# Strassen products of g @ w_out that add on in PSUM over several products, in another order, with the last tile copied in halves

## Chip, cores and metric

The kernel runs on one core of a Trainium2 chip. The metric is the device time of one execution in microseconds. Before the change it was 564.1 us, the median of three runs (562.77, 564.2 and 564.1 us).

## The reference

Attention with a capped score, then two two-layer networks one behind the other. Shapes: q, k, v are 2 x 12 x 448 x 64; x is 896 x 768, each w_in 768 x 2048, each w_out 2048 x 768 (held as 64-bit floats).

```
scores = cap * tanh(q @ k.T / 8 / cap)
attn   = softmax(scores);  x = attn @ v            # heads side by side: 896 x 768
h = x @ w_in1;   g = where(h > 0, h, exp(min(h, 0)) - 1);   x = g @ w_out1
h = x @ w_in2;   g = maximum(0.01 * h, h);                  out = g @ w_out2
```

## The kernel before

Everything runs transposed: an activation tile is 128 features x 448 tokens, one of two batches. Each fp32 operand is split into a high and a low part that TensorE takes in its fp32r format, and a product is three matmuls: high x high, high x low, low x high. ScalarE (ACT) makes the high part by a copy with rounding (`rounded`, L303), VectorE (DVE) the low part by a subtraction (`remainder`, L306).

The work has three stages: attention (pairs of heads, to some 116 us), then for each network the hidden layer (`hidden`, L632: 16 tiles of 128 features, 36 matmuls each at L646) and the output layer (`products`, L726).

The output layer is one level of Strassen's scheme in Winograd's form. g is cut into four quarters B11 to B22 (feature half x batch; 8 tiles of 128 features each), w_out into A11 to A22 (4 slabs of 128 x 768 each). Seven products of sums of quarters take the place of eight. Each product has 8 steps kt of 9 matmuls (3 output tiles m x 3 parts, L751), so 72 matmuls; a network has 504 of them.

- Names. `tl1.6.0` is the low part of B's operand in network 1, product 6, step 0; `th1.6.0` its high part; `S1.6.0l` and `S1.6.0h` the parts of A's operand (one for two steps). `gg1.3.0` is a tile of g (tile 3, batch 0), `w1.10.0` a slab of w_out (quarter A21, slab 0). `u` tiles hold sums of products, `c` tiles a finished quarter of the result.
- Operands. `operand` (L710) has DVE add or subtract two quarters in place (L718), 16 times on slabs and 32 times on g tiles for each network.
- Accumulators. Each product opens its own (`accumulators`, L610): a pair of PSUM banks `acc` for m = 0, 1 (tag `sc`, two of them) and one bank `acs` for m = 2 (tag `po`, two of them). So two products can be open at a time, and the third reopens the banks of the first.
- After a product (`after`, L771), for each m: products 7 and 1 are copied by ACT into u7 and u1 (L777); product 6 gives u2 = u1 + M6 and u7 = u7 + u2 (L781, L784); 5, 3, 4 and 2 give a quarter each by a DVE addition (L790), and 5 also u2 = u2 + M5 (L794). In network 1 a quarter is split into the parts `xh2`, `xl2` for the next hidden layer; in network 2 it is transposed on TensorE (`ct`, L809), copied out of PSUM and stored.
- The order of the products is 7, 1, 6, 5, 3, 4, 2. In the last one the last two steps are done m by m, so that the first tiles finish early.
- `convert` (L542) makes fp32 weights of the 64-bit ones; two of its steps are on ACT (L555, L567) and two on DVE (L576, L585).

No engine chooses its work at run time. `Plan` (L18) takes every piece with a cost, what it reads and writes and a due time, lists them engine by engine in an order worked out beforehand, and `order` (L73) hands them out; each engine then runs its own list strictly in turn and waits for semaphores where a piece needs another engine's result. Where two engines touch one PSUM tile, their accesses are kept apart by such a wait, two reads too.

Of the kernel before, what the change touches and what calls it, by code (L numbers as in the profile page):

```python
# [256 lines left out]
def block(ctx, tc, consts, q, k, v, w_in1, w_out1, w_in2, w_out2, out, bounded):  # L257
# [17 lines left out]
    P = 128  # L275
# [266 lines left out]
    def convert(key, src, name, tag, due):  # L542
# [16 lines left out]
        def low():  # L559
# [7 lines left out]
            nc.scalar.activation(x, top, AF.Identity, scale=1.0 / 32.0, bias=third)  # L567
# [64 lines left out]
    def hidden(nm, m, at):  # L632
# [76 lines left out]

    def operand(nm, p, side, idx):  # L710
        spec = PRODUCTS[p][side]
        if len(spec) == 1:
            return part(nm, side, spec[0], idx)
        x, op, y, to = spec
        x, y, to = (part(nm, side, pr, idx) for pr in (x, y, to))

        def fn():
            nc.vector.tensor_tensor(out=V[to], in0=V[x], in1=V[y], op=op)  # L718

        plan("DVE", (0.87, 0.54)[side], fn, reads=[x, y], writes=[to], port=True)  # L720
        return to
# [4 lines left out]
    def products(nm, T0):  # L726
        for j, p in enumerate(PRODUCTS):
            tags, where = accumulators(list(range(MS)))
            T = T0 + j * MS * 3 * (KF // 2) * MM
            s_of, t_of = {}, {}  # L730
            for kt in range(KF // 2):
# [10 lines left out]
                def fn(kts=(kt,), ms=range(MS), tags=tags, where=where, nm=nm, p=p):  # L742
                    if 0 in kts:
# [24 lines left out]
            for m in range(MS):  # L768
                after(nm, p, m, where[m], T + (KF // 2) * 9 * MM - (6 * MM * (MS - 1 - m) if p == 2 else 0))

    def after(nm, p, m, acc, T):  # L771
# [3 lines left out]
        free = T if p == 2 else T + 7.0  # L775
        if p in (7, 1):
# [10 lines left out]
        i, n, of, op = {2: (0, 0, 1, ADD), 3: (0, 1, 2, ADD), 4: (1, 0, 7, SUB), 5: (1, 1, 7, ADD)}[p]
        c = f"c{nm}.{i}{n}.{m}"
        home = "x" if p == 5 else "g"
        plan("DVE", 0.54, lambda: nc.vector.tensor_tensor(  # L790
            out=tl(home, home, c, [P, S]), in0=V[u(of)], in1=bank(acc), op=op),
            reads=[u(of), acc], writes=[c], new={c: home}, due=free + 2)
        if p == 5:
            plan("DVE", 0.54, lambda: nc.vector.tensor_tensor(out=V[u(2)], in0=V[u(2)], in1=bank(acc), op=ADD),  # L794
                 reads=[u(2), acc], writes=[u(2)], due=free + 3)
# [145 lines left out]
```

## Time and profile before

| | |
|---|---|
| timed runs | 562.77, 564.2, 564.1 us; median 564.1 us |
| profiled execution, first to last instruction | 560.4 us |
| median less that span | 3.7 us |
| TensorE (PE) busy | 550.4 us, 98% |
| weight loads (PEld, beside PE) | 452.7 us, 81% |
| DVE busy | 479.8 us, 86% |
| ACT busy | 385.8 us, 69% |

The profiled execution's own time is not listed beside its span; what a timed run has beyond the span lies before the first and after the last instruction. The granted TensorE clock is 1.00 in every window but the last (0.87 from 546 us on, where PE runs out of work), which is the 2.4 GHz level. Busy shares say which engine is full, not which one is waited for: DVE is busy for all of 238 to 280 us, and whether TensorE waits for it is seen in the waits.

### The profile page before, as it was taken

The numbers are of one execution on the slowest core, as the hardware profiler recorded it, in microseconds if no ns is written. First come the engines' busy times: TensorE is split into PE (matmuls) and PEld (weight loads), VectorE is DVE, ScalarE is ACT, GpSimd is POOL, SyncE is SP. The second block draws the span as 40 slices with busy tenths as digits, with TensorE's granted clock in tenths as the row PEclk, the third lists the DMA queues.
The fourth block names the chain that finished last, engine by engine and source line by source line (L and its number), as shares of the span: only waits on it lengthen the run. The fifth ranks groups of instructions, "written<-read, shape, count | busy, mean of one in ns | idle before, by whom it ended". The sixth has DMA issues, their size and how long they took to land.

```text
span 560.4 us, 7414 instructions
## 1 busy us (share of the span) xinstructions
PE 550.4 (98%) x2750; PEld 452.7 (81%) x2750; DVE 479.8 (86%) x628; ACT 385.8 (69%) x539; POOL 52.5 (9%) x32
## 2 busy tenths in 40 slices
PE   8999999999999999999999999999999999999995
PEld 4333433489999999999999999999999999999994
DVE  2699999987887999999999977888997599997662
ACT  5899999919877889865566766776775256555550
POOL 2544454500000000000000000000000000000000
PEclk9999999999999999999999999999999999999998
DMA  8933641155777667400012128676672000001103
GB/s 159 245 77 82 141 137 34 57 159 144 220 215 222 174 210 225 123 2 0 1 56 57 57 65 250 193 224 195 205 206 72 0 2 1 1 1 49 50 20 86
DMA packets 61436, 61.90 MB, mean 110 GB/s; under 512 B 23248, under 2 KB 53200, under 8 KB 61392
## 3 DMA queue, kind: packets, MB, share of 16 engines
q1 hardware_dynamic: 61120, 61.23, 39.3%
q8 instruction: 23, 0.38, 0.3%
q14 instruction: 21, 0.17, 0.1%
q10 hardware_dynamic: 240, 0.11, 0.1%
q0 software_dynamic: 32, 0.00, 0.0%
HBM read 58.59 MB, written 2.75 MB: 109 GB/s over the span
## 4 chain that ended last, share of the span: by engine, by line
PE 87%; DVE 5%; ACT 4%; POOL 1%; issue 1%; DMA 1%; SPq 0%; ACTq 0%; POOLq 0%
PE acc L646 29%; PE acc L751 24%; PE acs L751 12%; PE po L496 3%; DVE rec L516 2%; PE sm L510 1%; PE ct L809 1%; DMA firstq<-in_q_dram 1%; PE acs15.0_1845 L646 1%; PE acs38.0_3883 L646 1%; PE acs32.1_3492 L646 1%; PE acs9.1_1437 L646 1%; PE acs35.0_3687 L646 1%; PE acs29.1_3302 L646 1%; PE acs6.1_1242 L646 1%
## 5 line engine op out<-in xcount | busy, mean ns | idle before, releaser
L516 DVE RECIPROCAL rec<-sm 128x448 f32<-128x448 f32 x12 | 35.4, 2949 | 2.4 <-PE sm L510 2.2
L358 DVE COPY kT<-ntk 128x448 f32<-128x448 f32 x12 | 7.4, 619 | 6.7 <-PE ntk L343 6.6
L343 PEld LDWEIGHTS ntq<-ident,nq 112*128 112x128 f32 x44 | 4.3, 141 | 9.3 <-DVE kT L358 8.6
L343 PEld LDWEIGHTS ntk<-ident,nk 112*128 112x128 f32 x44 | 4.3, 141 | 7.3 <-issue 6.7
L354 DVE TENSOR_SCALAR qT<-ntq,qscale 128x448 f32<-128x448 f32 x12 | 8.1, 678 | 1.9 <-PE ntq L343 1.9
L829 ACT COPY ob<-ct 112x512 f32<-112x512 f32 x7 | 4.1, 587 | 7.4 <-PE ct L809 6.9
L343 PE MATMUL ntq<-ident,nq 112*128 112x112 f32 x44 | 6.6, 273 | 1.4 <-DVE kT L358 1.4
L524 DVE TENSOR_TENSOR xf<-po,rec 128x448 f32<-128x448 f32 x12 | 7.5, 623 | 0.4
L567 ACT ACTIVATE rawo1.00.2_972<-rawo1.00.2_972,third 128x768 int32<-128x768 uint8 x1 | 1.0, 1006 | 8.9 <-DMA rawo1.00.2_972<-in_moe_w_out_dram 8.9
L343 PE MATMUL ntk<-ident,nk 112*128 112x112 f32 x44 | 6.6, 273 | 0.0
L675 ACT ACTIVATE ea2.14.0_3955<-acs38.0_3883 128x448 f32<-128x448 f32 x1 | 0.5, 543 | 5.4 <-PE acs38.0_3883 L646 5.4
L303 ACT CAST th2.7.3_4004<-gg2.3.1_3278 128x448 fp32r<-128x448 f32 x1 | 0.6, 567 | 5.0 <-PE acs L751 5.0
L238 PE MATMUL unused<-busy 128*128 128x128 f32 x12 | 2.9, 435 | 1.1 <-DVE third L244 1.1
L391 ACT ACTIVATE e0.0_155<-sc0.0_147 112x896 f32<-112x896 f32 x1 | 0.9, 917 | 3.9 <-PE sc0.0_147 L371 3.9
L238 PEld LDWEIGHTS unused<-busy 128*128 128x128 f32 x12 | 2.6, 330 | 1.1 <-DVE third L244 1.1
L790 DVE TENSOR_TENSOR c2.00.0_4963<-u2.1.0_4297,acc 128x448 f32<-128x448 f32 x1 | 0.6, 622 | 3.2 <-PE acc L751 3.2
L660 ACT ACTIVATE ea1.0.0_1062<-acc 128x448 f32<-128x448 f32 x1 | 0.5, 547 | 4.1 <-PE acc L646 4.1
L827 DVE COPY ob<-ct 112x512 f32<-112x512 f32 x4 | 2.8, 690 | 0.7 <-PE ct L809 0.7
L666 DVE SCALAR_TENSOR_TENSOR gg1.0.0_1074<-ea1.0.0_1062,acc 128x448 f32<-128x448 f32 x1 | 0.6, 620 | 3.2 <-ACT ea1.0.0_1062 L663 3.2
L675 ACT ACTIVATE ea2.13.0_3904<-acc 128x448 f32<-128x448 f32 x1 | 0.5, 543 | 3.9 <-PE acc L646 3.9
L306 DVE TENSOR_TENSOR tl2.7.3_4006<-gg2.3.1_3278,th2.7.3_4004 128x448 fp32r<-128x448 f32 x1 | 0.6, 626 | 3.0 <-ACT th2.7.3_4004 L303 3.0
L263 DVE TENSOR_SCALAR ncap<-capb 128x1 f32<-128x1 f32 x1 | 0.2, 154 | 3.6 <-DMA capb<-in_cap_dram 3.6
(4976 smaller groups left out, 2263.9 us busy)
## 6 DMA issues: line engine op xcount, KB each, us to landing
nv<-in_v_dram SPq DMA_DIRECT2D x12, 224.0 KB, 3.0
nk<-in_k_dram SPq DMA_DIRECT2D x11, 224.0 KB, 3.6
nq<-in_q_dram SPq DMA_DIRECT2D x11, 224.0 KB, 3.8
out_dram<-ob SPq DMA_DIRECT2D x3, 672.0 KB, 4.3
rawg1.0_203<-in_moe_w_in_dram SPq DMA_DIRECT2D x1, 768.0 KB, 7.3
rawg1.1_248<-in_moe_w_in_dram SPq DMA_DIRECT2D x1, 768.0 KB, 6.0
rawg1.2_282<-in_moe_w_in_dram SPq DMA_DIRECT2D x1, 768.0 KB, 7.7
rawo1.00.0_514<-in_moe_w_out_dram SPq DMA_DIRECT2D x1, 768.0 KB, 5.6
```

Source lines behind the costliest of these rows:

```text
L238: nc.tensor.matmul(t, busy, busy, start=True, stop=True)
L343: nc.tensor.matmul(t[:, c * CP : (c + 1) * CP], V[f"n{nm}{n}"][:, c], ident[:CP, :CP], is_transpose=True, start=True, stop=True,)
L354: nc.vector.tensor_scalar(out=t, in0=V[pt][:, :S], scalar1=qscale, scalar2=None, op0=ALU.mult)
L358: nc.vector.tensor_copy(t, V[pt][:, :S])
L496: nc.tensor.matmul(V[po][j * D : (j + 1) * D, :S], V[f"nv{n}"][:, j, c], V[e][:, c % 2, j], start=(c == 0), stop=(c == NC - 1),)
L510: nc.tensor.matmul(t[j * D : (j + 1) * D, :S], ones[:CP], V[f"s{n}.0"][:, j], start=True, stop=True,)
L516: plan("DVE", 2.97, lambda: nc.vector.reciprocal(out=tl("att", "rec", rec, [P, S]), in_=V[sm][:, :S]), reads=[sm], writes=[rec], new={rec: ...
L524: nc.vector.tensor_tensor(out=tl("att", "xf", xf, [P, S]), in0=V[po][:, :S], in1=V[f"rec{n}"], op=ALU.mult)
L646: nc.tensor.matmul(bank(where[b]), V[g + w][:, kt, :], V[f"{part}{nm}.{b}.{kt}"], start=(x == 0 and i == 0), stop=(x == KM - 1 and i == 2),)
L751: nc.tensor.matmul(bank(where[m]), V[sp][:, kt % 2, m * P : (m + 1) * P], V[tp], start=(kt == 0 and i == 0), stop=(kt == KF // 2 - 1 and i ...
L809: nc.tensor.matmul(t[:CP, x * P : (x + 1) * P], V[c][:, x * CP : (x + 1) * CP], ident, is_transpose=True, start=True, stop=True,)
L829: nc.scalar.copy(dst, src)
```

## The change

Products that go into the same sum now share an accumulator, and the sum forms in PSUM. There are three: X takes M1, then M6, then M5, then M3; Y takes M7, then M4 (its operand is now B21 - B12 with the opposite sign, so that it adds); Z takes M2. The order is 1, 7, 6, 4, 5, 2, 3. `opens` says whether a product starts its accumulator or adds on. ACT copies the sum out where a later step needs it: u1 (after product 1), u7 (after 7) and u6 (X after product 6). Then c10 = u6 + Y, c11 = u7 + X, c00 = u1 + Z, each one DVE addition for each m; c01 is X itself after product 3 and needs none. The additions of L781, L784 and L794 are gone.

In network 1 c01 is split into its parts straight from PSUM. In network 2 it is copied out first: m = 0 by ACT, m = 1 by DVE, and m = 2, the last tile, in two halves of 224 columns, one by each. In `convert` the step L567 is now a Copy with a constant for its bias, where it was Identity with the bias read from a tile.

```diff
-            nc.scalar.activation(x, top, AF.Identity, scale=1.0 / 32.0, bias=third)
+            nc.scalar.activation(x, top, AF.Copy, scale=1.0 / 32.0, bias=-15.5 / 32.0)
...
-        7: ((A11, SUB, A21, A21), (B22, SUB, B12, B12)),
-        1: ((A11,), (B11,)),
...
+        1: (A11, (), B11, (), "X"),
+        7: (A21, ((A11, SUB, A21, A21),), B12, ((B22, SUB, B12, B12),), "Y"),
+        6: (A21, ((A22, SUB, A21, A21),), B12, ((B12, ADD, B11, B12),), "X"),
+        4: (A22, (), B12, ((B22, SUB, B12, B11), (B21, SUB, B12, B12)), "Y"),
...
+    FINAL = {4: (1, 0, 6), 5: (1, 1, 7), 2: (0, 0, 1), 3: (0, 1, None)}
+    LAST = 3
...
-            tags, where = accumulators(list(range(MS)))
+            opens = PRODUCTS[p][4] not in sums
+            if opens:
+                sums[PRODUCTS[p][4]] = accumulators(list(range(MS)))
+            tags, where = sums[PRODUCTS[p][4]]
...
-                                    start=(kt == 0 and i == 0), stop=(kt == KF // 2 - 1 and i == 2),
+                                    start=(opens and kt == 0 and i == 0), stop=(kt == KF // 2 - 1 and i == 2),
...
-        if p in (7, 1):
+        if p not in FINAL:
             plan("ACT", 0.46, lambda: nc.scalar.copy(tl("x", "x", u(p), [P, S]), bank(acc)),
...
-            plan("DVE", 0.54, lambda: nc.vector.tensor_tensor(out=V[u(7)], in0=V[u(7)], in1=V[u(2)], op=ADD),
...
-            plan("DVE", 0.54, lambda: nc.vector.tensor_tensor(out=V[u(2)], in0=V[u(2)], in1=bank(acc), op=ADD),
...
+        last = p == LAST and m == MS - 1
+        halves = [(c, 0, S)]
+        if last:
+            halves = [(c + "a", 0, S // 2), (c + "b", S // 2, S)]
+        if of is None:
+            for x, (name, a, z) in enumerate(halves):
+                by = ("ACT", "DVE")[(m + x) % 2]
```

What this does to the lists of the engines is shown at three places. TensorE's list keeps its shape: the same count of matmuls at each line, and the same places at which a step of the next product comes ahead of the last step of the one before; only the operands' names differ.

First DVE in network 1, the stretch that ends with the first low part of the fourth product (product 5 before, product 4 in the change). Before, it reads:

```order
L306 TENSOR_TENSOR tl1.6.4_2324<-gg1.4.1_1294,th1.6.4_2319 128x448
L306 TENSOR_TENSOR S1.6.3l<-w1.10.3_1403,S1.6.3h 128x768
L718 TENSOR_TENSOR w1.10.1_1267<-w1.01.1_1839,w1.10.1_1267 128x768
L306 TENSOR_TENSOR tl1.6.5_2342<-gg1.5.1_1366,th1.6.5_2339 128x448
L718 TENSOR_TENSOR w1.10.2_1331<-w1.01.2_1906,w1.10.2_1331 128x768
L306 TENSOR_TENSOR tl1.6.6_2358<-gg1.6.1_1432,th1.6.6_2353 128x448
L306 TENSOR_TENSOR S1.5.0l<-w1.00.0_607,S1.5.0h 128x768
L718 TENSOR_TENSOR w1.10.3_1403<-w1.01.3_1937,w1.10.3_1403 128x768
L718 TENSOR_TENSOR gg1.0.1_1080<-gg1.0.1_1080,gg1.8.0_1569 128x448
L306 TENSOR_TENSOR tl1.5.0_2390<-gg1.0.0_1074,th1.5.0_2371 128x448
```

Here the additions on slabs of w stand between the parts of product 6. In the change the same stretch reads:

```order
L306 TENSOR_TENSOR S1.6.3l<-w1.10.3_1415,S1.6.3h 128x768
L306 TENSOR_TENSOR tl1.6.5_2335<-gg1.5.1_1378,th1.6.5_2331 128x448
L718 TENSOR_TENSOR gg1.4.0_1300<-gg1.12.1_1825,gg1.4.1_1302 128x448
L718 TENSOR_TENSOR gg1.4.1_1302<-gg1.12.0_1815,gg1.4.1_1302 128x448
L306 TENSOR_TENSOR tl1.6.6_2352<-gg1.6.1_1444,th1.6.6_2347 128x448
L306 TENSOR_TENSOR S1.4.0l<-w1.11.0_1482,S1.4.0h 128x768
L718 TENSOR_TENSOR gg1.5.0_1370<-gg1.13.1_1892,gg1.5.1_1378 128x448
L718 TENSOR_TENSOR gg1.5.1_1378<-gg1.13.0_1888,gg1.5.1_1378 128x448
L718 TENSOR_TENSOR gg1.6.0_1442<-gg1.14.1_1962,gg1.6.1_1444 128x448
L306 TENSOR_TENSOR tl1.4.0_2385<-gg1.0.1_1080,th1.4.0_2365 128x448
```

The additions on slabs of w have moved out of this stretch, and the additions on g for the two operands of product 4 have come in, two for each tile. From the first low part of product 6 to that of the next product DVE has 9 instructions on 768 columns and 13 on 448 before, and 4 and 21 in the change.

Second ACT in network 1, in the fourth product. Before, its list reads:

```order
L303 CAST S1.5.1h<-w1.00.1_813 128x768
L303 CAST th1.5.1_2407<-gg1.1.0_1121 128x448
L303 CAST th1.5.2_2422<-gg1.2.0_1179 128x448
L303 CAST th1.5.3_2438<-gg1.3.0_1219 128x448
L303 CAST S1.5.2h<-w1.00.2_1024 128x768
L303 CAST th1.5.4_2457<-gg1.4.0_1292 128x448
L303 CAST S1.5.3h<-w1.00.3_1135 128x768
```

It holds high parts alone. In the change the list reads:

```order
L303 CAST th1.4.3_2430<-gg1.3.1_1231 128x448
L303 CAST S1.4.2h<-w1.11.2_1627 128x768
L782 COPY u1.6.0_2437<-acc_1975 128x448
L782 COPY u1.6.1_2450<-acc_1975 128x448
L303 CAST th1.4.4_2452<-gg1.4.1_1302 128x448
L303 CAST S1.4.3h<-w1.11.3_1697 128x768
L782 COPY u1.6.2_2457<-acs_1976 128x448
L303 CAST th1.4.5_2470<-gg1.5.1_1378 128x448
```

The three copies u1.6 of accumulator X have come in among the high parts. The buffer `acc_1975` that they read is the one that product 1 opened and that product 5 adds to next.

Third the end of the program, with what each instruction waits for (a suffix _49 belongs to the semaphore's name). ACT's list before is:

```order
L829 COPY ob_4887<-ct_4905 112x4x128 [waits PE_49]
L303 CAST th2.2.6_4934<-gg2.14.0_3959 128x448 [waits DVE_49,PE_49]
L303 CAST th2.2.7_4936<-gg2.15.0_4022 128x448 [waits PE_49,Activation_49]
L829 COPY ob_4985<-ct_4973 112x4x128 [waits DMAHW4_49,PE_49]
L829 COPY ob00.0_4995<-ct_4989 112x256 [waits PE_49]
```

The last two rows copy transposed tiles out of PSUM. In the change ACT's list is:

```order
L303 CAST th2.3.7_4902<-gg2.15.1_4000 128x448 [waits PE_49,Activation_49]
L813 COPY c2.01.0_4929<-acc_3962 128x448 [waits PE_49]
L813 COPY c2.01.2a<-acs_3963 128x224 [waits PE_49]
L844 COPY ob_4953<-ct_4939 112x4x128 [waits DMAHW4_49,PE_49]
L844 COPY ob01.0_4963<-ct_4957 112x256 [waits PE_49]
```

Two copies of the quarter's own tiles have come in ahead of them. DVE's list before is:

```order
L306 TENSOR_TENSOR tl2.2.7_4949<-gg2.15.0_4022,th2.2.7_4936 128x448 [waits PE_49,Activation_49]
L790 TENSOR_TENSOR c2.00.0_4963<-u2.1.0_4297,acc_4837 128x448 [waits PE_49]
L790 TENSOR_TENSOR c2.00.1_4971<-u2.1.1_4310,acc_4837 128x448
L790 TENSOR_TENSOR c2.00.2_4978<-u2.1.2_4321,acs_4838 128x448 [waits PE_49]
L827 COPY ob_4985<-ct_4980 112x4x128 [waits DMAHW4_49,PE_49]
L827 COPY ob00.2_4997<-ct_4989 112x256 [waits Activation_49]
```

Three additions make the quarter's tiles. In the change DVE's list is:

```order
L306 TENSOR_TENSOR tl2.3.6_4913<-gg2.14.1_3945,th2.3.6_4900 128x448 [waits DVE_49,PE_49,Activation_49]
L306 TENSOR_TENSOR tl2.3.7_4915<-gg2.15.1_4000,th2.3.7_4902 128x448 [waits PE_49,Activation_49]
L815 COPY c2.01.1_4937<-acc_3962 128x448 [waits Activation_49]
L815 COPY c2.01.2b<-acs_3963 128x224 [waits Activation_49]
L842 COPY ob_4953<-ct_4948 112x4x128 [waits DMAHW4_49,PE_49]
L842 COPY ob01.2_4965<-ct_4957 112x256 [waits Activation_49]
```

The last quarter's three additions on DVE have become a copy of m = 0 on ACT, one of m = 1 on DVE that waits for ACT, and two halves of m = 2, of which DVE's waits for ACT's. ACT's copy of the transposed tile m = 0 (`ob` from `ct`) now stands behind two copies more.

## Rows read from the trace of the kernel before

**Rows 1.** The page, part 1: busy time, share of the span, instructions.

```profile
PE 550.4 (98%) x2750; PEld 452.7 (81%) x2750; DVE 479.8 (86%) x628; ACT 385.8 (69%) x539; POOL 52.5 (9%) x32
```

**Rows 2.** PE's waits, first and last of six: us in total, times, longest.

```profile
PE ntq L343 <- DVE kT L358: 1.4, 3, 0.7
...
PE ct L809 <- ACT ob L829: 0.2, 1, 0.2
```

**Rows 3.** Windows of 14 us: busy time (instructions), granted clock, DMA share, GB/s.

```profile
core 0: us, PE busy (x) PEld busy (x) DVE busy (x) ACT busy (x) POOL busy (x), PEclk, DMA share, GB/s
...
252.00:266.00 14.00, 14.00 (x70) 12.97 (x70) 14.00 (x23) 8.00 (x15) 0.00 (x0) 1.00 0.00 0
...
476.00:490.00 14.00, 14.00 (x71) 12.97 (x70) 14.00 (x22) 8.14 (x15) 0.00 (x0) 1.00 0.01 1
...
546.00:561.00 15.00, 8.20 (x45) 7.16 (x44) 4.05 (x7) 1.21 (x3) 0.00 (x0) 0.87 0.31 87
```

**Rows 4.** Chain of waits in network 1: start, us, engine, tile, line, count.

```profile
245.90 1.21 PE acc L751 x6
247.72 1.22 PE acc L751 x6
```

**Rows 5.** Timeline of DVE: start, us, line, operation, tile written and tiles read.

```profile
252.45 0.95 DVE L718 TENSOR_TENSOR w1.00.2_1024<-w1.10.2_1331,w1.00.2_1024 128x768 f32<-128x768 f32 x1
253.32 0.62 DVE L306 TENSOR_TENSOR tl1.6.0_2250<-gg1.0.1_1080,th1.6.0_2233 128x448 fp32r<-128x448 f32 x1
253.86 0.62 DVE L306 TENSOR_TENSOR tl1.1.7_2252<-gg1.7.0_1497,th1.1.7_2235 128x448 fp32r<-128x448 f32 x1
```

**Rows 6.** Timeline at the head of product 5, network 2: maker and first user.

```profile
487.59 0.62 DVE L306 TENSOR_TENSOR tl2.5.0_4383<-gg2.0.0_3078,th2.5.0_4365 128x448 fp32r<-128x448 f32 x1
...
488.53 0.36 PE L751 MATMUL acc<-tl2.5.0_4383,S2.5.0h 128*128 128x448 f32 x1
```

**Rows 7.** Line L777: duration min/median/max in ns, first and last start.

```profile
L777 ACT COPY u1.7.0_2166<-acc x1: 525/525/525, 245.1 to 245.1; 128x448 f32<-128x448 f32 x1
...
L777 ACT COPY u1.7.2_2188<-acs x1: 539/539/539, 247.2 to 247.2; 128x448 f32<-128x448 f32 x1
```

**Rows 8.** Timeline of PE: the third product's first matmul.

```profile
254.86 0.36 PE L751 MATMUL acc<-th1.6.0_2233,S1.6.0h 128*128 128x448 f32 x1
```

**Rows 9.** Timeline at the start of the second network: maker and first user.

```profile
331.78 0.62 DVE L306 TENSOR_TENSOR xl2.0.0_3002<-c1.00.0_2988,xh2.0.0_2991 128x448 fp32r<-128x448 f32 x1
...
333.69 0.36 PE L646 MATMUL acc<-xl2.0.0_3002,g2.0h 128*128 128x448 f32 x1
```

**Rows 10.** Timeline of the end of the program.

```profile
551.10 0.36 PE L751 MATMUL acc<-th2.2.7_4936,S2.2.3l 128*128 128x448 f32 x1
...
551.50 0.62 DVE L790 TENSOR_TENSOR c2.00.0_4963<-u2.1.0_4297,acc 128x448 f32<-128x448 f32 x1 [3.24 <-PE acc L751]
...
552.31 0.36 PE L751 MATMUL acs<-th2.2.7_4936,S2.2.3l 128*128 128x448 f32 x1
...
552.51 0.60 PE L809 MATMUL ct<-ident,c2.00.0_4963 128*112 128x128 f32 x4
552.71 0.62 DVE L790 TENSOR_TENSOR c2.00.2_4978<-u2.1.2_4321,acs 128x448 f32<-128x448 f32 x1
...
553.15 0.58 ACT L829 COPY ob<-ct 112x512 f32<-112x512 f32 x1 [6.90 <-PE ct L809]
...
553.79 0.65 PE L809 MATMUL ct<-ident,c2.00.2_4978 128*112 128x128 f32 x4 [0.24 <-ACT ob L829]
554.47 0.37 ACT L829 COPY ob00.0_4995<-ct 112x256 f32<-112x256 f32 x1 [0.74 <-PE ct L809]
...
554.88 0.42 DVE L827 COPY ob00.2_4997<-ct 112x256 f32<-112x256 f32 x1 [0.60 <-ACT ob00.0_4995 L829]
```

**Rows 11.** The page, part 5: DVE copies of 128 x 448 out of PSUM.

```profile
L358 DVE COPY kT<-ntk 128x448 f32<-128x448 f32 x12 | 7.4, 619 | 6.7 <-PE ntk L343 6.6
```

**Rows 12.** Line L567, one of its conversions.

```profile
L567 ACT ACTIVATE rawo1.00.2_972<-rawo1.00.2_972,third x1: 1006/1006/1006, 120.6 to 120.6; 128x768 int32<-128x768 uint8 x1
```

**Rows 13.** Line L555, the conversion's other step on ACT.

```profile
L555 ACT ACTIVATE w1.00.2_1024<-rawo1.00.2_972 x1: 902/902/902, 121.9 to 121.9; 128x768 f32<-128x768 f32 x1
```

More of the change, by code (lines that the diff above doesn't have):

```diff
@@ L710, in operand, with fn @@
     def operand(nm, p, side, idx):
[L711 to L721, printed above, removed]
+        for x, op, y, to in PRODUCTS[p][2 * side + 1]:
+            x, y, to = (part(nm, side, pr, idx) for pr in (x, y, to))
+            def fn(x=x, op=op, y=y, to=to):
+                nc.vector.tensor_tensor(out=V[to], in0=V[x], in1=V[y], op=op)
+            plan("DVE", (0.87, 0.54)[side], fn, reads=[x, y], writes=[to], port=True)
+        return part(nm, side, PRODUCTS[p][2 * side], idx)
     us = {}
@@ L779, in after @@
             return
-        if p == 6:
+        i, n, of = FINAL[p]
+        c = f"c{nm}.{i}{n}.{m}"
+        if of is not None:
             plan("DVE", 0.54, lambda: nc.vector.tensor_tensor(
-                out=tl("x", "x", u(2), [P, S]), in0=V[u(1)], in1=bank(acc), op=ADD),
-                reads=[u(1), acc], writes=[u(2)], new={u(2): "x"}, due=free + 2)
-            plan("DVE", 0.54, lambda: nc.vector.tensor_tensor(out=V[u(7)], in0=V[u(7)], in1=V[u(2)], op=ADD),
-                 reads=[u(7), u(2)], writes=[u(7)], port=True, due=free + 5)
-            return
@@ L787, in after @@
[L787 to L793, printed above, removed]
-            plan("DVE", 0.54, lambda: nc.vector.tensor_tensor(out=V[u(2)], in0=V[u(2)], in1=bank(acc), op=ADD),
-                 reads=[u(2), acc], writes=[u(2)], due=free + 3)
+                out=tl("g", "g", c, [P, S]), in0=V[u(of)], in1=bank(acc), op=ADD),
@@ L796, in after @@
+                reads=[u(of), acc], writes=[c], new={c: "g"}, due=free + 2)
         if nm == "1":
             hi, lo = f"xh2.{n}.{3 * i + m}", f"xl2.{n}.{3 * i + m}"
[L798 to L801 removed]
@@ L802, in after @@
-            return
+            src = acc if of is None else c
+            x = (lambda: bank(acc)) if of is None else (lambda: V[c])
+            plan("ACT", 0.46, lambda: rounded(tl("x", "x", hi, [P, S], F32R), x()),
+                 reads=[src], writes=[hi], new={hi: "x"}, due=free + 4)
+            plan("DVE", 0.54, lambda: nc.vector.tensor_tensor(
+                out=tl("x", "x", lo, [P, S], F32R), in0=x(), in1=V[hi].bitcast(F32), op=SUB),
+                reads=[src, hi], writes=[lo], new={lo: "x"}, port=of is not None, due=free + 6)
@@ new lines, in after, with copy @@
+            return
+        last = p == LAST and m == MS - 1
[5 more added lines that the diff above has]
+                by = ("ACT", "DVE")[(m + x) % 2]
+                def copy(name=name, a=a, z=z, by=by):
+                    to = tl("g", "g", name, [P, S])[:, : z - a]
+                    src = bank(acc)[:, a:z]
+                    if by == "ACT":
+                        nc.scalar.copy(to, src)
+                    else:
+                        nc.vector.tensor_copy(to, src)
+                plan(by, 0.5 * (z - a) / S + 0.1, copy, reads=[acc], writes=[name], new={name: "g"}, due=free + 1)
@@ L808, in transpose @@
             for x in range(NC):
+                name, a, _ = next(h for h in halves if h[1] <= x * CP < h[2])
                 nc.tensor.matmul(
-                    t[:CP, x * P : (x + 1) * P], V[c][:, x * CP : (x + 1) * CP], ident,
+                    t[:CP, x * P : (x + 1) * P], V[name][:, x * CP - a : (x + 1) * CP - a], ident,
                     is_transpose=True, start=True, stop=True,
                 )
-        plan("PE", 0.45, transpose, reads=[c], writes=[pt], new={pt: tag}, at=T + (1.5 if p != 2 else 6 * MM * (MS - 1 - m) + 0.5 + 0.5 * m))
-        last = p == 2 and m == MS - 1
+        plan("PE", 0.45, transpose, reads=[h[0] for h in halves], writes=[pt], new={pt: tag},
+             at=T + (1.5 if p != LAST else 6 * MM * (MS - 1 - m) + 0.5 + 0.5 * m))
         def evacuate(engine, cs):
@@ L851, in after @@
              new={ob: "raw"} if m == 0 else None)
-        ms = [m] if p == 2 else list(range(MS)) if m == MS - 1 else []
+        ms = [m] if p == LAST else list(range(MS)) if m == MS - 1 else []
         if ms:
```

28 lines of the change are left out of this document (12 added, 16 removed).

## Prediction, made before the change was run

> **What bounds the kernel now.** I read the busy shares first: TensorE has work for 98% of the span [rows 1]. That alone does not say that nothing waits, so the view of PE's waits comes second. It lists six, 3.9 us in all: 1.4, 1.1, 0.5, 0.4 and 0.3 us for attention's transposes and inputs, and 0.2 us for a transpose at the very end [rows 2]. None is at the lines of the hidden layers or the products. The chain of waits shows the same as a rhythm: the nine matmuls of one step kt take from 245.90 to 247.72 us, 1.82 us or 0.202 us each, step after step [rows 4], at full granted clock [rows 3]. A product of 72 matmuls thus takes 14.6 us, and the 1008 matmuls of the two output layers 204 us whatever the other engines do, as long as operands are there in time.
>
> DVE looks like the bound in the windows 252 to 266 and 476 to 490 us, where it is busy for all 14.00 us [rows 3]. It is full and nearly late, but not late. The nearest miss that I found is the low part tl2.5.0: DVE starts it at 487.59 and ends 0.62 us later, at 488.21; TensorE uses it at 488.53 [rows 6], 0.32 us later. So in this execution DVE's work costs nothing, and what DVE is spared gains nothing by itself.
>
> **The change part by part.** TensorE's own work stays: 1152 matmuls at the hidden layers' line, 1008 at the products', 48 transposes of results, in the same places of its list. Whether a matmul starts a sum or adds to it changes no count. Term: 0.
>
> *DVE is spared 22 instructions.* Before there are 24 additions that make quarters, and 6 + 6 + 6 that make u2 and u7; in the change 18 additions and 2 copies. A DVE instruction of 448 columns shows 0.62 us, but the next starts 0.54 us after it, and one of 768 columns 0.87 us after (253.32 to 253.86, and 252.45 to 253.32) [rows 5]. So 22 x 0.54 = 11.9 us leave DVE's list, all beside TensorE's matmuls. Term: 0, bounded by what DVE's lateness costs TensorE now, which is nothing.
>
> *DVE's work is moved.* The 32 additions on quarters of a network stay, but product 4 needs two on each g tile, which fall into products 6 and 4. By the counts of the lists, from the first low part of product 6 to that of the next product there are 9 instructions on 768 and 13 on 448 columns before: 9 x 0.87 + 13 x 0.54 = 14.9 us. In the change 4 and 21: 14.8 us. In the next product it is 4 and 21 before (14.8 us), 10 and 11 in the change (14.6 us). TensorE's product is 14.6 us, so DVE falls behind there by 0.3 and 0.2 us before, and by 0.2 and 0.0 us in the change. Network 1's margins thus stay, and network 2, where the thinnest margin is, loses the u additions ahead of its fourth product. Term: 0; the list is as full as it was, not fuller. If this cover were gone, each 0.1 us of DVE lateness at the head of a product would be 0.1 us of TensorE standing still.
>
> *ACT gets 8 copies more:* three for u6 in each network, 0.53 us each [rows 7], and the two of the last quarter. ACT works 8.00 and 8.14 us in the two windows where DVE is full [rows 3], so 1.6 us more in a product of 14.6 us has room. The instructions behind a copy on ACT are high parts, for which DVE waits and then TensorE.
>
> *Shared accumulators.* A product that adds on must wait until ACT has copied the sum so far. That is a wait with another cause, but at the place of an old one: before, the third product reopens the first one's banks and waits for the very same copies. There u7's copies run from 245.1 to 247.2 + 0.54 = 247.7 us [rows 7], and the third product's first matmul starts at 254.86 [rows 8]: 7.1 us to spare. X and Y alternate up to product 5, Z takes Y's banks, and 3 adds on X, so a whole product always lies between. What used to be DVE's reads of the banks of product 6 is now ACT's copies u6, which stand ahead of product 4's last three high parts in ACT's list. Term: 0.
>
> *From network 1 to 2.* The last quarter loses its additions: ACT rounds from PSUM, DVE subtracts from PSUM. Before, xl2.0.0 starts at 331.78, ends at 332.40 and is used at 333.69, 1.3 us later [rows 9]. One step of some 0.6 us goes from that chain; against that the tile's reads by ACT and DVE now wait for one another. Term: 0 either way, since TensorE has other tiles to work on until then.
>
> *The end.* The last matmuls of m = 0, 1 and of m = 2 end at 551.10 + 0.36 = 551.46 and at 552.67 us [rows 10]. Before, DVE's addition makes m = 2 from 552.71 to 553.33. But its transposes start only at 553.79: they wait for ACT's copy of the transposed m = 0 (553.15 + 0.58 = 553.73), which holds their PSUM bank. In the change, ACT copies m = 0 by 551.50 + 0.53 = 552.03, and DVE m = 1 from 552.07, for 0.62 us [rows 11], to 552.69. ACT copies its half of m = 2 from 552.72; the nearest row is the 0.37 us for 256 columns [rows 10], so it ends by 553.09, before the transposed m = 0 is there (552.51 + 0.60 = 553.11). DVE's half waits for ACT's and takes 0.42 us at most [rows 10]: 553.13 to 553.55. That is 0.22 us later than before and still ahead of 553.73. Term: 0. Bounds: nothing below zero, as the bank's holder has not moved; above, if each half took as long as a whole copy (0.53 and 0.62 us), ACT's half would end at 553.25 and put off its next copy by 0.10 us, and DVE's would end at 553.91, so the transposes start some 0.2 us late. I take 0, the nearest rows being those of 256 columns.
>
> The trace shows two engines reading one PSUM tile in turn: ACT's output copy ends at 554.84 and DVE's of the same tile starts at 554.88 [rows 10]. The Trainium skill, page "PSUM — Partial Sum Buffer", section "PSUM bank collisions raise a hardware error", says that two engines on one bank and the same partitions collide, reads against reads too, so software must keep them apart. It speaks against halving the last tile, and the trace agrees. By that rule m = 2 is ready at 553.55; halves side by side would have it at 553.14.
>
> *The conversion's Copy.* The step L567 takes 1.01 us with its bias from a tile, and the other ACT step of the same columns, which reads no bias, 0.90 us [rows 12, 13]. I take between 0 and 0.1 us less for each of 61, on an engine that has room. Term: 0.
>
> **Sum.** 560.4 us of span + 0 = 560.4 us. The timed median is 3.7 us above that span, 564.1 us; nothing in the change touches what lies around the span. Forecast: 564.1 us, no change.
>
> **Rivals.** *DVE gets late (slower).* Its place is the head of the products from the second to the fifth. In their stretches it has 14.5 to 14.9 us of work for TensorE's 14.6, and the pairs of additions on one g tile depend on the low part just before them. If such handoffs (0.04 us from one engine to the next, 554.84 to 554.88) added 0.5 us to each of three products, 1.5 us of lateness would come up against a margin of about 0.9 us: TensorE stands still for 0.6 us in each network, and with the same once more in the two products behind it loses some 2 us: 566. It decides from a lateness of one margin on. For it: the thin margins. Against it: DVE's total there is no higher than before.
>
> *Lateness that this profile missed is removed (faster, but little).* The timed runs differ by 1.4 us. If the slower ones held stalls at heads such as that of product 5, the change would remove them, and all runs would be at the lowest one, 562.8 us. Against it: no such stall in the profile.
>
> *The end gets shorter.* If the halves ran side by side and ACT's next copy did not matter, the transposes could start at about 553.4 and not at 553.79: 0.4 us, 563.7. The bank speaks against it, and so does the wait in DVE's list.
>
> *It comes out clearly faster:* for that TensorE would have to do the same matmuls in less time, below 562.4; no row shows how.
>
> **How the numbers follow.** What a measurement of this kernel can tell from no change is about 0.3%, 1.7 us. Forecast 72%, DVE late 11%, lateness removed 9%, shorter end 3%, clearly faster 5%. The second and third rivals stay within 0.3%. So: faster 0.05, same 0.84, slower 0.11. Range: 562.4 to 565.6 us; below it lies the clearly faster case and above it most of DVE's lateness.
>
> **What would show it.** Right: PE's waits name no line of the products, one step kt stays at 1.82 us, DVE's busy time falls by about 12 us, ACT's grows by some 4 us less what the conversions save, and the transposes of the last tile still wait for ACT. Wrong: a wait of PE for a low part (DVE late), for a copy u6 (shared accumulators), or a start of the last transposes other than 1.1 us after the last matmul's end.

## Result and the profile after

The change makes the kernel slower: 568.69 us (565.45 to 569.12, 6 executions) against 563.51 us (562.77 to 564.47, 6), ratio 1.0076 with an interval of [1.0056, 1.0096]. The forecast was 564.1 us and the range ended at 565.6 us. The profiled execution took 568.55 us with a span of 566.8 us, 6.4 us more than the span before.

The page's busy shares and the first and last of PE's waits in the profile after:

```profile
PE 557.2 (98%) x2750; PEld 453.7 (80%) x2750; DVE 470.2 (83%) x606; ACT 384.2 (68%) x547; POOL 52.7 (9%) x32
```

```profile
PE ntq L343 <- DVE kT L358: 1.4, 3, 0.7
...
PE ct L825 <- ACT ob L844: 0.2, 1, 0.2
```

By these two views nothing has happened that was not forecast: the same number of matmuls, DVE 9.6 us lighter, no wait of PE at the products [rows 1, 2]. But PE is busy for 6.8 us more with the same 2750 instructions. Where, the chain of waits shows. Its columns are start, length, engine, tile, line, count; each row is one step kt, of which it lists the six matmuls on `acc`:

```profile
267.17 1.22 PE acc L755 x6
269.00 1.22 PE acc L755 x6
271.04 1.29 PE acc L755 x5
272.95 1.24 PE acc L755 x6
274.81 1.24 PE acc L755 x6
```

Up to 269.00 a step starts 1.82 or 1.83 us after the one before, as in the kernel before [rows 4]. From 272.95 on it is 1.86 us: 0.2067 us from one matmul's start to the next (called the pitch below) in place of 0.2027. This holds to 514.59 us, where the transposes of finished results come between the products. It holds in network 2's hidden layer too, whose code is the same in both kernels. The windows say it in instructions; the first answers to one of [rows 3], and so does the third:

```profile
core 0: us, PE busy (x) PEld busy (x) DVE busy (x) ACT busy (x) POOL busy (x), PEclk, DMA share, GB/s
252.00:266.00 14.00, 14.00 (x71) 12.96 (x70) 13.93 (x23) 8.11 (x15) 0.00 (x0) 1.00 0.00 1
280.00:294.00 14.00, 14.00 (x69) 12.71 (x69) 14.00 (x21) 8.26 (x14) 0.00 (x0) 1.00 0.14 39
476.00:490.00 14.00, 14.00 (x70) 12.71 (x68) 13.93 (x24) 8.14 (x15) 0.00 (x0) 1.00 0.01 2
```

PE is full in all three. The weight loads (PEld), of equal length each, are the better counter: 12.96 us of them fit into 14 us before the step and 12.71 us behind it, at a granted clock of 1.00 in every window. From 271.55 us to the transposes at 514.59 us there are 1176 matmuls of this pitch; at 0.0040 us each that is 4.7 us.

What stands at the step is in the timeline around 271 us (all engines, rows picked):

```profile
268.64 0.62 DVE L718 TENSOR_TENSOR gg1.5.0_1370<-gg1.13.1_1892,gg1.5.1_1378 128x448 f32<-128x448 f32 x1
...
269.29 0.62 DVE L718 TENSOR_TENSOR gg1.5.1_1378<-gg1.13.0_1888,gg1.5.1_1378 128x448 f32<-128x448 f32 x1
...
269.84 0.62 DVE L718 TENSOR_TENSOR gg1.6.0_1442<-gg1.14.1_1962,gg1.6.1_1444 128x448 f32<-128x448 f32 x1
...
270.37 0.62 DVE L306 TENSOR_TENSOR tl1.4.0_2385<-gg1.0.1_1080,th1.4.0_2365 128x448 fp32r<-128x448 f32 x1
...
270.66 0.36 PE L755 MATMUL acc<-th1.4.0_2365,S1.4.0h 128*128 128x448 f32 x1
...
271.04 0.19 PEld L755 LDWEIGHTS acc<-tl1.4.0_2385,S1.4.0h 128*128 128x128 f32 x1 [0.40 <-DVE tl1.4.0_2385 L306]
271.04 0.47 PE L755 MATMUL acc<-tl1.4.0_2385,S1.4.0h 128*128 128x448 f32 x1
```

This is the head (the first step) of product 4 of network 1. DVE ends the low part tl1.4.0 at 270.99; its matmul should have started 0.2 us after the one of 270.66 and starts 0.39 us after it. So TensorE stands still for 0.18 us. PE's own waits don't show it, since the matmul of 270.66 ends, as modelled, at 271.02 and the next one begins at 271.04; it stands as 0.40 us on the line of the weight loads. The kernel before has a margin of 0.93 us at the same head, from the low part's end (268.10 + 0.62 = 268.72) to the matmul (269.65):

```profile
268.10 0.62 DVE L306 TENSOR_TENSOR tl1.5.0_2390<-gg1.0.0_1074,th1.5.0_2371 128x448 fp32r<-128x448 f32 x1
269.45 0.19 PEld L751 LDWEIGHTS acc<-tl1.5.0_2390,S1.5.0h 128*128 128x128 f32 x1
269.65 0.36 PE L751 MATMUL acc<-tl1.5.0_2390,S1.5.0h 128*128 128x448 f32 x1
```

Two distances in these rows are used below: a weight load starts 0.20 us ahead of its matmul (269.45 and 269.65), and where the operand is late, the load starts 0.05 us after the operand is ready (270.99 and 271.04).

Two smaller parts make up the rest of the 6.4 us. At the very start the same transposes and scores take longer (upper rows: before, lower rows: after; PE's timeline from 4 us on):

```profile
4.34 0.57 PE L343 MATMUL ntk<-ident,firstk 112*128 112x112 f32 x4 [0.35 <-DMA firstk<-in_k_dram]
...
6.63 1.01 PE L371 MATMUL sc0.0_147<-qT,kT 64*112 64x448 f32 x4 [0.54 <-DVE qT L354]
```

```profile
4.28 0.98 PE L343 MATMUL ntk<-ident,firstk 112*128 112x112 f32 x4 [0.30 <-DMA firstk<-in_k_dram]
...
7.08 1.84 PE L371 MATMUL sc0.0_147<-qT,kT 64*112 64x448 f32 x4 [0.32 <-DVE qT L354]
```

The first matmul of the hidden layer comes at 108.92 us, before at 107.71: 1.2 us. The code there is the same, and the kernel before has both starts as well (last experiment), so these 1.2 us do not belong to the change; the rest is 5.2 us, as is the difference of the two medians. From the first matmul on `acc` to the last matmul of the products it is 449.56 us, before 444.60: 5.0 us, which are the stall of 0.18 us, the 4.7 us of pitch and 0.1 us that the second matmul behind the stall comes late (271.04 to 271.35). Behind the last one it is 0.2 us more. The end itself, answering to [rows 10]:

```profile
558.88 0.35 ACT L813 COPY c2.01.2a<-acs 128x224 f32<-128x224 f32 x1 [0.68 <-PE acs L755]
...
559.26 0.39 DVE L815 COPY c2.01.2b<-acs 128x224 f32<-128x224 f32 x1 [0.41 <-ACT c2.01.2a L813]
559.32 0.59 ACT L844 COPY ob<-ct 112x512 f32<-112x512 f32 x1
...
559.96 0.43 PE L825 MATMUL ct<-ident,c2.01.2a 128*112 128x128 f32 x2 [0.24 <-ACT ob L844]
```

The halves run one after the other and the transposes wait for ACT's copy of `ob`: 559.96 is 1.12 us behind the last matmul's end (558.48 + 0.36), before 553.79 - 552.67 = 1.12.

### The profile page after: what moved, and what is told of

Read it like the earlier page. It is cut to its first block, busy times and chain, and to the rows that moved or that the text cites. A ratio compares the mean times of both kernels' runs of the same rounds, so it can differ in the third digit from the quotient of the medians.

```text
span 566.8 us, 7397 instructions
## 1 busy us (share of the span) xinstructions
PE 557.2 (98%) x2750; PEld 453.7 (80%) x2750; DVE 470.2 (83%) x606; ACT 384.2 (68%) x547; POOL 52.7 (9%) x32
## 4 chain that ended last, share of the span: by engine, by line
PE 88%; DVE 5%; POOL 2%; ACT 2%; issue 2%; DMA 1%; POOLq 0%; ACTq 0%
PE acc L646 29%; PE acc L755 24%; PE acs L755 12%; PE po L496 3%; DVE rec L516 2%; PE sm L510 1%; PE ct L825 1%; PE ntq L343 1%; PE acs34.1_3862 L646 1%; PE acs34.0_3861 L646 1%; PE acs31.1_3674 L646 1%; PE acs31.0_3673 L646 1%; PE acs28.1_3487 L646 1%; PE acs28.0_3486 L646 1%; PE acs25.1_3295 L646 1%
## 5 line engine op out<-in xcount | busy, mean ns | idle before, releaser
L567 ACT ACTIVATE rawo1.00.2_972<-rawo1.00.2_972 128x768 int32<-128x768 uint8 x1 | 0.9, 929 | 8.9 <-DMA rawo1.00.2_972<-in_moe_w_out_dram 8.9
```

## Experiments

Three theories. **T1:** a low part that is late at a product's head breaks TensorE's stream of loads and matmuls, and the stream falls into a pitch of 0.2067 us until something else breaks it. **T2:** matmuls that add to an open sum, or the banks they use, are slower in themselves. **T3:** ACT's constant or the halved last tile costs it. Every run was timed beside 31 to 35 executions of the kernel before (median 563.85 to 564.03 us, none above 565.01). Behind a time stand its lowest and highest execution and their number, then the ratio to the kernel before with its interval. Whether the longer pitch is there is seen in the profiled execution alone; for the others it is inferred from the time.

**Three operations of VectorE moved, to make tl1.4.0 earlier** (after):
```
+    move("DVE", ("gg1.6.0", "gg1.6.1", "gg1.14.1"), "tl1.6.7")
+    for x in (1, 0):
+        move("DVE", (f"w1.10.{x}", f"w1.01.{x}"), "S1.5.3l")
```


> The kernel after, with VectorE's list changed at one place: the in-place addition on gg1.6.0 for product 4 and the two additions that make w1.10.1 and w1.10.0 stand later, so that tl1.4.0 is ready about 0.5 us earlier than the matmul that reads it wants it. T1 (a short stall of TensorE at tl1.4.0 in product 4 puts its matmuls into a slower rhythm, 0.2067 us each instead of 0.2027, until the transposes of network 2): no gap at 271 us, 0.2027 us per matmul from there on, 563.4 to 564.2 us. T2 (matmuls that add to an open sum are slower in themselves, or the bank is): the 0.2067 us stays, 568 to 569 us. T3 (the ScalarE copy or the halved last tile costs it): 568 to 569 us.

Measured: 564.88 us (562.88 to 565.66, 10), 1.0019 [1.0001, 1.0036]. tl1.4.0 is ready 0.42 us ahead of its matmul, and 0.2027 us holds to network 2. Another head (tl1.2.0, at 300.98) now stalls by 0.36 us, and the pitch survives that. So the longer pitch isn't in the adding matmuls, and a stall does not always bring it.

**A stall put into the kernel before:**
```
+    for x in ("gg1.14.0", "gg1.15.0"):
+        nc.vector.tensor_tensor(out=V[x], in0=V[x], in1=V[x], op=ALU.max)   # ahead of tl1.5.0
```


> The kernel before, with two VectorE operations that change nothing (maximum of a g tile with itself, 0.54 us each) put ahead of tl1.5.0 in product 4, where the profile before left 0.93 us. T1: TensorE waits 0.1 to 0.3 us there once, and then goes at 0.2067 us per matmul until the transposes of network 2: 567.5 to 569 us. T2 and T3: nothing but the stall, 563.5 to 564.3 us.

Measured: 564.73 us (562.72 to 569.56, 10), 1.0030 [1.0000, 1.0059]. Two of ten executions came out at 568.45 and 569.56 us, the others at 562.7 to 565.0. In the profiled one TensorE stalls by 0.19 us, the weight loads at the next two heads come 0.20 and 0.13 us late, and 0.2027 us stays. Neither theory had it so: under T1, a late low part sets the longer pitch in part of the executions only.

**Four transposes two steps behind the stall** (after):
```
+    for x in range(4):   # ahead of the first matmul that reads tl1.4.2; result not used
+        nc.tensor.matmul(t[:CP, x*P:(x+1)*P], busy[:, :CP], ident, is_transpose=True, start=True, stop=True)
```


> The kernel after, with four transposes (of a constant, into the score bank, nobody reads them) in TensorE's list two steps behind the stalled matmul, ahead of the first matmul that reads tl1.4.2. T1 with transposes as what ends the slow rhythm: 0.2067 us per matmul for some microseconds only, then 0.2027 us again, 0.3 us for the transposes, 563.9 to 564.8 us. T2 and T3: the 0.2067 us stays, 568.5 to 569.5 us.

Measured: 564.74 us (563.05 to 565.53, 10), 1.0018 [1.0003, 1.0033]. Windows of its profile between stall and transposes, and behind them:

```profile
272.00:276.50 4.50, 4.50 (x24) 4.08 (x23) 4.50 (x8) 2.13 (x4) 0.00 (x0) 1.00 0.01 4
278.00:282.50 4.50, 4.50 (x24) 4.17 (x23) 4.50 (x7) 2.61 (x5) 0.00 (x0) 1.00 0.00 0
```

The stall is there (0.18 us at tl1.4.0), the longer pitch follows it (4.08 us of loads in 4.5 us), and the four transposes end it (4.17 us). All of it lies in one execution, with sums that add on either side. T1 fits, T2 does not.

**ACT's constant and the whole last tile restored** (after):
```
-            nc.scalar.activation(x, top, AF.Copy, scale=1.0 / 32.0, bias=-15.5 / 32.0)
+            nc.scalar.activation(x, top, AF.Identity, scale=1.0 / 32.0, bias=third)
-        if last:
-            halves = [(c + "a", 0, S // 2), (c + "b", S // 2, S)]
```


> The kernel after, with ScalarE's constant read from a tile again and the last tile copied whole, as in the kernel before; the products and their order stay those of after. T1 and T2: 568 to 569 us, with 0.2067 us per matmul from 271 us on. T3: 563.2 to 564.2 us.

Measured: 566.30 us (562.71 to 568.83, 10), 1.0039 [1.0010, 1.0069]. Five of ten lie between 567.5 and 568.9 us, five between 562.7 and 565.1. The profiled one has the stall (0.18 us at 271.82) but not the pitch. T3 falls: the longer times come without both edits.

**The kernel after once more:**

> The kernel after once more, unchanged, beside the three others. T1 as it stands after the first four runs: the stall at tl1.4.0 comes in every execution, the slower rhythm (0.2067 us per matmul) in part of them: two groups of times, near 563 to 565 us without it and near 567.5 to 569 us with it, more than one in four in the second group. T2 (the adding matmuls are slow in themselves): all near 568 us.

Measured: 567.85 us (564.40 to 569.34, 12), 1.0064 [1.0043, 1.0085]; nine of twelve above 567 us. With the six executions of the result that is 14 of 18. Its trace holds a finding: the stall at tl1.4.0 is there (0.18 us) and the pitch stays at 0.2027; it turns at the next head, where no matmul is late. The weight loads there:

```profile
286.02 0.19 PEld L755 LDWEIGHTS acc<-th1.5.0_2502,S1.5.0h 128*128 128x128 f32 x1
286.30 0.19 PEld L755 LDWEIGHTS acc<-tl1.5.0_2520,S1.5.0h 128*128 128x128 f32 x1
286.43 0.19 PEld L755 LDWEIGHTS acc<-th1.5.0_2502,S1.5.0l 128*128 128x128 f32 x1
```

A load otherwise follows the last one after 0.20 us. This one comes after 0.28 us, because tl1.5.0 was ready 0.18 us ahead of its matmul and the load needs it 0.20 + 0.05 = 0.25 us ahead. The matmul still starts on time (0.205 us after the one before it), and from there on the pitch is 0.2067.

**A stall of 1.3 us in the kernel before** (four of the added operations instead of two):

> The kernel before with four VectorE operations that change nothing ahead of tl1.5.0 in product 4: a stall of about 1.2 us in place of the 0.2 us of the run with two. T1 if any stall can set the slow rhythm: two groups of times, 564 to 566 us and 568.5 to 570.5 us. T1 if only stalls of some 0.2 us can: one group, 564 to 566 us. T2: one group as well.

Measured: 568.61 us (564.23 to 570.62, 10), 1.0080 [1.0055, 1.0106]; six of ten from 568.2 us up, the others at 564.2 to 566.5. So the longer times come without a single sum that adds on. The profiled execution (565.44 us) keeps 0.2027, and behind its stall the loads at the next two heads are late by 0.21 and 0.13 us, so it is not shown that it was the long stall, and not one of these, that set the pitch in the six.

**The pairs of additions taken apart** (after):
```
+    for first, second, behind in (("gg1.1.1", "gg1.9.0", "tl1.6.2"), ("gg1.2.1", "gg1.10.0", "tl1.6.3"),
+            ("gg1.4.1", "gg1.12.0", "tl1.6.6"), ("gg1.5.1", "gg1.13.0", ("gg1.6.0", "gg1.14.1")), ...
+        move("DVE", (first, second), behind)
```


> The kernel after, with VectorE's list changed only where two additions on one g tile stood side by side (the second writes the tile that the first reads): one other operation now stands between the two, at four places ahead of tl1.4.0 in network 1 and three in network 2. If the pairs are what made VectorE late: each such addition 0.54 us instead of 0.65, tl1.4.0 ready 0.4 us earlier, no stall at 271 us, 0.2027 us per matmul from first product to last in every execution, 562.6 to 564.8 us. If they are not: stall and times as in the kernel after, part of them 567.5 to 569 us.

Measured: 564.02 us (562.37 to 564.54, 12), 0.9995 [0.9983, 1.0007]. DVE's timeline in this run, with one of the pairs and the first low parts of products 6 and 4:

```profile
253.88 0.62 DVE L306 TENSOR_TENSOR tl1.6.0_2244<-gg1.0.1_1080,th1.6.0_2227 128x448 fp32r<-128x448 f32 x1
...
257.42 0.62 DVE L718 TENSOR_TENSOR gg1.1.0_1121<-gg1.9.1_1652,gg1.1.1_1125 128x448 f32<-128x448 f32 x1
257.96 0.62 DVE L306 TENSOR_TENSOR tl1.6.2_2277<-gg1.2.1_1185,th1.6.2_2275 128x448 fp32r<-128x448 f32 x1
258.49 0.62 DVE L718 TENSOR_TENSOR gg1.1.1_1125<-gg1.9.0_1648,gg1.1.1_1125 128x448 f32<-128x448 f32 x1
...
268.60 0.62 DVE L306 TENSOR_TENSOR tl1.4.0_2385<-gg1.0.1_1080,th1.4.0_2365 128x448 fp32r<-128x448 f32 x1
```

In the kernel after the second of two neighbours comes 0.65 us behind the first (268.64, 269.29 above), here each comes 0.54 us behind the last. From tl1.6.0 to tl1.4.0 DVE takes 14.72 us here and 15.22 us in the kernel after (255.15 to 270.37), so the four pairs cost 0.50 us. Without them the low part is ready 0.37 us ahead of its matmul in place of 0.13 us too late. All twelve executions are level with the kernel before. So the lateness is the cause: with it 14 of 18 executions have the longer time, without it none of 12 here and none of 36 in the runs below that keep the pairs apart. Seven instructions moved by one place each undo the whole loss.

**Two heads of network 2 cleared as well** (gg2.6.0 behind tl2.6.7, w2.10.2 behind tl2.4.7):

> As the run with the pairs apart, and two more VectorE operations moved in network 2, so that tl2.4.0 and tl2.5.0 (0.06 us of margin each, 0.1 us of stall in the kernel after) are ready 0.5 us and 0.9 us earlier. T1: no product stalls at its head, 562.4 to 564.6 us, level with the kernel before. T2: 567.5 to 569 us in part or all.

Measured: 563.92 us (562.15 to 565.25, 12), 0.9999 [0.9985, 1.0012]. The run shows nothing beyond the last one: with the pairs apart the two heads had margins of 0.43 and 0.32 us already. (The 0.06 us that was expected of them is seen in the runs that keep 0.2027; in the profiled executions of the kernel after TensorE goes slower there and they have 0.74 and 0.92 us.)

**A thin margin without a stall, in the kernel before:**
```
+    for x, n in (("gg1.14.0", S), ("gg1.15.0", 112)):
+        nc.vector.tensor_tensor(out=V[x][:, :n], in0=V[x][:, :n], in1=V[x][:, :n], op=ALU.max)
```


> The kernel before with one full and one narrow VectorE operation that change nothing (0.54 us and about 0.2 us) ahead of tl1.5.0 in product 4, whose margin falls from 0.93 us to about 0.2 us, so that no matmul starts late. T1 with a real stall as the trigger: all executions 562.5 to 564.8 us. T1 with the margin as the trigger (the slower rhythm came at a margin of 0.18 us in the second look at the kernel after): part of the executions 567 to 569.5 us.

Measured: 564.11 us (562.26 to 568.91, 12), 1.0013 [0.9991, 1.0035]; three of twelve from 566.8 us up, and one of them is the profiled one. At tl1.5.0 the margin is 0.21 us as planned; the weight load comes 0.05 us late and the pitch stays. At the next head it is 0.10 us. Weight loads, then matmuls there:

```profile
285.36 0.19 PEld L751 LDWEIGHTS acc<-th1.3.0_2512,S1.3.0h 128*128 128x128 f32 x1
285.72 0.19 PEld L751 LDWEIGHTS acc<-tl1.3.0_2530,S1.3.0h 128*128 128x128 f32 x1 [0.17 <-DVE tl1.3.0_2530 L306]
```

```profile
285.77 0.42 PE L751 MATMUL acc<-tl1.3.0_2530,S1.3.0h 128*128 128x448 f32 x1
286.03 0.37 PE L751 MATMUL acc<-th1.3.0_2512,S1.3.0l 128*128 128x448 f32 x1
286.24 0.37 PE L751 MATMUL acc<-th1.3.0_2512,S1.3.0h 128*128 128x448 f32 x1
```

The load waits 0.17 us, one matmul comes 0.06 us late, and the pitch is 0.2067 us up to the transposes at 514.40. The kernel before now spends 449.05 us from the first matmul on `acc` to the last matmul of the products, in place of 444.60, with its own products. That rules T2 out. A loss of 0.06 us was paid with 4.4 us.

**Transposes in the kernel before, without a wait:**

> The kernel before with four transposes ahead of the first matmul that reads tl1.5.2, no stall at their place: a break in TensorE's stream without a wait. T1 with waits alone as the trigger: 0.3 us for the transposes, 562.7 to 565.1 us in every execution. If any break in the stream can set the slower rhythm: part of them 567.5 to 569.5 us.

Measured: 563.93 us (562.83 to 565.10, 10), 1.0007 [0.9993, 1.0021]. A break without a wait set no longer pitch at this place. At another it does, and T1 as stated is too narrow: in the trace of before the eight transposes of results from 508.40 us on wait for nothing, and behind them the longer pitch holds until the next four, at 511.12:

```profile
508.83 0.60 PE L809 MATMUL ct<-ident,c2.11.1_4568 128*112 128x128 f32 x4
...
509.68 0.37 PE L751 MATMUL acc<-th2.3.2_4549,S2.3.1l 128*128 128x448 f32 x1
...
510.92 0.36 PE L751 MATMUL acs<-th2.3.2_4549,S2.3.1l 128*128 128x448 f32 x1
511.12 0.60 PE L809 MATMUL ct<-ident,c2.11.2_4570 128*112 128x128 f32 x4
```

Six matmuls take 1.24 us there, 0.2067 each. Nine of the fourteen traces have these 2 us. So transposes end the longer pitch at some places and set it at others.

**More products of zeros at the start.** Leaving out the longer pitch, the times of every kernel fall into two groups, near 562.5 and near 564.3 us; of the kernel before 13 of 35 executions are in the lower one. This is the start seen above: of the profiled executions whose time is on record, those with first scores of 1.01 us took 562.2 to 563.0 us, and those with 1.84 us 564.15 us and more. Two versions of the run with the heads cleared:
```
-IDLE_PRODUCTS = 6
+IDLE_PRODUCTS = 7     # first version: 8, and three instead of one ahead of the first scores
```


> The run with the heads cleared, and more products of zeros at the very start: eight instead of six ahead of the first transposes, three instead of one ahead of the first scores. Executions of every kernel here fall into two groups 1.8 us apart by how fast TensorE goes between 4.3 and 8.5 us. If a busier TensorE brings the fast start more often: most executions 562.2 to 563.2 us, median about 1 us under the kernel before. If not: 563.9 to 564.9 us, 0.4 us for the added products on top.

> The run with the heads cleared, and seven products of zeros instead of six ahead of the first transposes, nothing else. If a busier TensorE brings the fast start more often: more than half of the executions at 562.2 to 563.2 us. If not: two groups as before, 562.2 to 563.2 and 563.7 to 565.2 us, median near 563.9 us.

Measured: 562.89 us (562.23 to 563.58, 12), 0.9987 [0.9978, 0.9997], for eight and three; 562.47 us (562.09 to 563.45, 12), 0.9982 [0.9971, 0.9993], for seven. All 24 executions lie below 563.7 us, where the upper group begins, 19 of them at 563.2 us or less. PE's timeline with seven:

```profile
3.14 1.27 PE L238 MATMUL unused<-busy 128*128 128x128 f32 x5
4.71 0.58 PE L343 MATMUL ntk<-ident,firstk 112*128 112x112 f32 x4 [0.30 <-PE unused L238]
...
6.70 1.01 PE L371 MATMUL sc0.0_148<-qT,kT 64*112 64x448 f32 x4 [0.54 <-DVE qT L354]
```

TensorE works to 4.41 us instead of some 3.99 and then does the transposes in 0.58 us and the scores in 1.01, as in the lower group. The median is 1.4 us under that of the kernel before; the added product owes nothing to the change in the products, and it was not tried in the kernel before.

## Why the prediction was wrong

*What bounds the kernel, and TensorE's own work: 0.* The count was right, 2750 instructions. But "a product of 72 matmuls takes 14.6 us whatever the other engines do" took the pitch for a constant. It has two values, 0.2027 and 0.2067 us (14.6 and 14.9 us per product), and in every trace here it changes only behind a late weight load or a run of transposes. This term should have been +4.7 us in most executions.

*DVE's work is moved: "Network 1's margins thus stay".* **This step failed first.** It compared DVE's totals per product, 14.9 and 14.8 before with 14.8 and 14.6. These take every instruction at 0.54 or 0.87 us. Two neighbours of which the second overwrites what the first reads are 0.65 us apart, or 0.98 us on 768 columns: 0.12 us more. The margin at product 4's head went from 0.93 us to 0.13 us too late: 1.06 us. In product 6's stretch, counted at 14.8 us, DVE took 15.22 us for its four pairs of additions; the run with the pairs apart shows these 0.50 us. The stretch ahead of it was not worked out, and the margin at product 6's head was already 0.49 us in place of 1.12. From the second product's first low part to the third's DVE took 15.14 us in place of 14.45: 0.2 us by its counts (7 instructions on 768 and 16 on 448 columns in place of 8 and 14), the rest by four more such neighbours. DVE's first low parts of the second and third product, one such pair and the third product's matmul (all after):

```profile
240.01 0.62 DVE L306 TENSOR_TENSOR tl1.7.0_2105<-gg1.0.1_1080,th1.7.0_2089 128x448 fp32r<-128x448 f32 x1
...
242.49 0.62 DVE L306 TENSOR_TENSOR tl1.7.1_2125<-gg1.1.1_1125,th1.7.1_2122 128x448 fp32r<-128x448 f32 x1
243.14 0.62 DVE L718 TENSOR_TENSOR gg1.1.1_1125<-gg1.1.1_1125,gg1.1.0_1121 128x448 f32<-128x448 f32 x1
...
255.15 0.62 DVE L306 TENSOR_TENSOR tl1.6.0_2244<-gg1.0.1_1080,th1.6.0_2227 128x448 fp32r<-128x448 f32 x1
...
256.26 0.37 PE L755 MATMUL acc<-tl1.6.0_2244,S1.6.0h 128*128 128x448 f32 x1
```

Before, neither stretch has such neighbours, but its trace has them elsewhere at the same 0.65 us. For the second half this is read from the rows; no run took these four apart.

*"Each 0.1 us of DVE lateness would be 0.1 us of TensorE standing still".* Wrong by more than an order of magnitude: 0.18 us of standing still cost 4.9 us, and 0.06 us in the kernel before cost 4.4 us. The margin itself was measured from the wrong point. I took it to the matmul; the weight load needs the low part 0.25 us ahead of the matmul. The Trainium skill, page "TensorE: Matmul & The Clock Gate", section "Architectural detail: the array is 16× 32×32, not 1× 128×128", says that TensorE can pull weight loads ahead of matmuls under way; the trace agrees, with loads 0.2 us ahead. So the 0.32 us of [rows 6] were really 0.07 us.

*The rival "DVE gets late" had the place and most of the cause:* the heads of the products, and additions that depend on what stands just before them. Its 0.5 us per product was measured in two products, not in three, and between neighbours on DVE itself, not in handoffs between engines. Its 2 us of stalls were 0.18 us in the profiled execution, and it has no change of pitch. The Trainium skill, page "VectorE: DVE Perf Modes", section "The DRAIN you can't avoid", says of eight chained copies that a semaphore after each one cost nothing extra. Here two neighbours of which the second waits for the first are 0.65 us apart, others 0.54; the measurement decides.

*What held.* DVE was spared 9.6 us (11.9 worked out), which moved no end. No product waited for a copy of a shared sum. The end came as worked out, 1.12 us; DVE's half waits for ACT's by the program's own order, so no run shows what two engines on one bank at once would do. The conversion's step of [rows 12] fell from 1006 to 929 ns, inside the bounds of 0 and 0.1 us, on an engine with room (line L567 after):

```profile
L567 ACT ACTIVATE rawo1.00.2_972<-rawo1.00.2_972 x1: 929/929/929, 121.7 to 121.7; 128x768 int32<-128x768 uint8 x1
```

*The 1.2 us at the start* was in the rival on the spread of the timed runs, which I took for stalls at the heads. It is the start. The sum has it too: every other profiled execution took 1.8 to 1.9 us more than its span, so about half of the 3.7 us between median and span is the fast start of that one execution, inside the span and not around it.

What stays open: why the stream has these two pitches, and what decides at a break which one follows. At a like stall of 0.18 us the pitch turned at once in two profiled executions of the kernel after and its variants and stayed in two others.

## What to carry to other kernels

Where an engine is full with a periodic stream, measure its pitch per instruction in windows before and after, and count in the weight loads: a busy share of 98% hid a pitch that was 2% longer. An operand must be ready when its weight load needs it (here 0.25 us ahead of the matmul); read the waits on that line as well, and work out each head's margin in the new order, with the price of dependent neighbours, rather than totals. Put one instruction between two on VectorE of which the second overwrites what the first reads.

## What was not expected of the hardware

- A stream of 128x128 weight loads and matmuls of 448 columns runs at 0.2027 or 0.2067 us per matmul at a granted clock of 1.00, and keeps either for over 1000 matmuls. A late weight load, by 0.08 us in one trace, turned it; one late by 0.07 us in another did not.
- Four transposes (0.35 us) turned it back in one trace; eight transposes without a wait set the longer pitch for 2 us in nine.
- Two neighbours on VectorE of which the second overwrites what the first reads start 0.65 us apart at 448 columns, others 0.54 us.
- The first matmuls of the program ran at 1.84 or 1.01 us per four of 448 columns, with a granted clock of 1.00 shown for 4 to 9 us in both. TensorE had done 12 matmuls of zeros up to 3.99 us and waited 0.3 to 0.6 us; two more of them, up to 4.41 us, brought times below 563.5 us in all 12 executions, with 1.01 us in the profiled one.
